# Infini-attention on one core: O formed with features on partitions

## The chip, the core and the metric

The kernel runs on one core of one Trainium2 chip. The core has a matrix engine (TensorE, PE in the profile; its weight loads are listed as PEld), three engines for elementwise work (VectorE or DVE, ScalarE or ACT, GpSimd or POOL), a sync engine (SP) that here issues nearly all transfers, and 16 DMA engines that carry them. The metric is device time in microseconds (us), lower is better. Three runs of the kernel before took 1043.05, 1041.55 and 1040.16 us, median 1041.55.

## The reference

Input `x` has 2048 tokens of 640 features. Two branches, A and B, each with weights of its own, apply the same memory-augmented attention to it, and a gate for each token mixes them. There are 32 heads of 20 features, and 4 segments of 512 tokens. Everything is float32.

```
q, k, v = x @ wq, x @ wk, x @ wv                # then cut into 32 heads and 4 segments
phi(t) = t + 1 if t > 0 else exp(t);  g = sigmoid(beta)          # one beta for each head
M = 0; z = 0
for each segment:
    p     = softmax(q k^T * 20**-0.5 + causal mask)
    a_dot = p v
    a_mem = (phi(q) M) / (phi(q) z + 1e-6)
    o     = g * a_mem + (1 - g) * a_dot
    M += phi(k)^T v;  z += sum of phi(k)
branch = o @ wo
gate = sigmoid(sum(x * gate_w));  out = gate * A + (1 - gate) * B
```

## The kernel before

The work is eight tiles: tile t is branch t % 2 of segment t // 2. A tile is cut into eight units of four heads, so 64 units in all, numbered 8t + u. TensorE's 128 rows are used as two halves of 64, each with a stream of its own; a product of 128 contracted rows is two records in the trace, one for each half. The 640 features are KT = 5 blocks of 128, the 512 tokens of a segment NB = 4 blocks of 128. Products that need more than the fast float format take three terms (high by high, high by low, low by high), so most operands are kept as a high and a low row.

The order of the work is set by a planner inside the program. It simulates the engines with a price for each instruction, and emits each engine's list in the order in which its own simulation comes to it. The table `RULES` gives for each unit the order of score and softmax pieces and how far they are spread. On the chip each engine works through its list in order, and waits by semaphores. Buffers are held in stores: eight banks of PSUM (128x512), `NBIG` = 27 rows of SBUF (128x512, called `row` in the trace), four quads each of q and k.

What a tile goes through, with the lines of the profile:

- Products of q, k, v and of the result (L643). q and k come out with features on partitions and go to DRAM (`qd`, `kd`, L625); from there SP loads them again by quads of four heads (`qst`, `kst`, L1032, 60 of 64 rows in each half). v goes to `vst[t % 2]`, tokens on partitions, 21 columns a head: 20 features and a one.
- Scores for the maxima (L1074), whose maxima VectorE takes (L1061). The maxima are turned (L1099), written into rows of `qst` (L1111), and the scores are formed once more, transposed (L1164), put through the exponential on ScalarE (L1156) and masked on GpSimd (L1157).
- PV (L1184): for each unit a bank with queries in the columns and, in four strips of 32 partitions, each head's 20 features and the row sum. The bank is copied to a row (L1209).
- `fin_unit`: four blocks, two halves, so eight transposes (L790) turn that row back to tokens on partitions; VectorE forms the weight gate x (1 - g) / row sum and multiplies (L1248 to L1250). For segments after the first GpSimd adds the memory's part (L1259).
- `mem_unit` (L752, from the third tile on): phi(q) x [M, z], for each of four token blocks and two groups of heads, with 128 tokens in the output's partitions and at most 84 columns per matmul. VectorE forms the weights, inverts them and multiplies into `Ot` (L766 to L769).
- `o_transpose`: for each of five blocks eight transposes (L790) turn O to features on partitions; it is split into high and low (L1277) for the product with wo.
- `back_unit` turns phi(k) (L790, L806), and `update_unit` adds phi(k)^T v to M and z (L830), held in `mbd`.

Where products are called for in a tile's stretch of the program is set by `window_jobs(t)`: first the rest of tile t's own products (`TAIL`), then the five O products of tile t - 1, then the first five of tile t + 1 (`HEAD`). Score, softmax, PV and transposing pieces are placed between them.

```
def window_jobs(t):
    got = [(t, kind, m) for kind, m in (TAIL if t else [("q", 1), ("k", 1), ("v", 0), ("q", 2), ("k", 2)] + TAIL[2:])]
    if t > 0:
        got += [(t - 1, "o", m) for m in range(KT)]
    if t < 7:
        got += [(t + 1, kind, m) for kind, m in HEAD]
    return got
```

Of the kernel before, what the change touches and what calls it, by code (L numbers as in the profile page):

```python
# [18 lines left out]
P = 128  # L19
# [15 lines left out]
OWN = [LO[m] if m == 0 else HI[m - 1] + 1 for m in range(KT)]  # L35

# [6 lines left out]
def tile_gated_mix_infini_attn(  # L43
# [47 lines left out]
        0: "TSTSTSTSTS 1.010 2.38 0.30 8",  # L91
        2: "TTSTSTSTSS 1.023 2.38 0.30 8",
        3: "TSTSTSTSTS 1.047 2.38 0.28 8",
        4: "TSTSTSTSTS 1.010 2.38 0.30 8",
        6: "TSSTTSSTTS 1.010 2.92 0.30 8",
        7: "TSTTSSTSTS 1.010 2.38 0.30 8",
        8: "TSTSTSTSTS 0.962 1.77 0.30 8",
        10: "TSTSTSTSTS 1.008 2.38 0.28 6",
        11: "TSTSTSTSTS 1.010 2.38 0.30 8",
        14: "TSTSTSTSTS 0.947 3.18 0.35 8",  # L100
        15: "TSTSTSTSTS 0.974 2.38 0.32 8",
        17: "TSSTTSSTTS 1.042 2.38 0.26 8",
        18: "TSTSTSTSTS 1.010 2.38 0.30 4",
        20: "TSTSTSTSTS 1.010 2.38 0.30 8",
        21: "SSTSTSTSTT 0.982 2.38 0.30 8",
        22: "TSTSTSTSTS 0.922 2.38 0.27 8",
        23: "TSTSTSTSTS 1.029 2.38 0.30 6",
        24: "TTSTSTSTSS 1.034 2.98 0.30 8",
        25: "TSTSTSTSTS 1.010 2.38 0.42 8",
        27: "SSTSTSTSTT 1.010 3.22 0.30 6",  # L110
        29: "TSTSTSTSTS 1.010 2.38 0.30 8",
        30: "SSSTSTSTTT 1.015 2.38 0.29 8",
        32: "TSTSTSTSTS 0.939 3.51 0.30 8",
        33: "TSTSTSTSTS 1.010 2.38 0.30 8",
        38: "TSTSTSTSTS 1.010 2.38 0.30 4",
        39: "TSTSTSTSTS 1.010 3.32 0.30 8",
        42: "STSTSTSTST 1.010 2.38 0.33 8",
        43: "TSTSTSTSTS 1.010 2.38 0.30 8",
        44: "TTSSTTSSTS 1.010 1.91 0.30 8",
        45: "TSTSTSTSTS 1.010 2.38 0.30 8",  # L120
        47: "TSTSTSTSTS 1.010 2.22 0.30 8",
        48: "TSTSTSTSTS 1.010 2.38 0.30 8",
        52: "TSTSTSTSTS 1.010 2.08 0.30 8",
        53: "SSTSTSTSTT 1.011 1.87 0.30 4",
        54: "TSTSTSTSTS 1.010 2.38 0.30 8",
        55: "TSTSTSTSTS 1.010 2.38 0.28 8",
        56: "TSTSTSTSTS 1.010 2.38 0.33 8",
        57: "TSTSTSTSTS 1.010 2.38 0.30 8",
        58: "TSTTSSTSTS 0.960 2.38 0.31 8",
        60: "TSTSTSTSTS 1.010 2.38 0.35 8",  # L130
        61: "TSTSTSTSTS 1.010 2.38 0.30 8",
        62: "TSTSTSTSTS 1.010 2.73 0.30 8",
        65: "TSTSTSTSTS 0.996 2.38 0.30 6",
    }
    rule = {}
    DONE = {"A": 0.14, "D": 0.11, "G": 0.1, "S": 0.0}
# [4 lines left out]
    def start_next(e):  # L141
# [7 lines left out]
        _, _, dur, emit, then = heapq.heappop(ready[e])  # L149
# [3 lines left out]
        def end():  # L153
            busy[e] = False
            load[e] -= dur
            if then:
                at(clk[0] + DONE[e], then)
            start_next(e)
# [10 lines left out]
    def put(e, dur, emit, then=None, prio=5):  # L169
        heapq.heappush(ready[e], (prio, next(seq), dur, emit, then))  # L170
        load[e] += dur
        start_next(e)
# [29 lines left out]
    lane = [0.0, 0.0]  # L202
    lane_ops = [deque(), deque()]
# [3 lines left out]
    def whole(dur, emit):  # L207
        now[0] = max(now[0], lane[0], lane[1]) + dur
        got = emit()
        lane[:] = [now[0], now[0]]  # L210
        advance(now[0])
        return got
# [4 lines left out]
    def op(half, dur, emit):  # L217
        now[0] = max(now[0], lane[half])
        advance(now[0])
        got = emit()  # L220
        lane[half] = now[0] + dur
# [44 lines left out]
    mbds = [[const.tile([P, HI[m] - LO[m] + 1, E1], F32, name=f"mbd{b}_{m}") for m in range(KT)] for b in range(2)]  # L266
# [1272 lines left out]
```

## Time and profile before

| | |
|---|---|
| median of three runs | 1041.55 us (1040.16 to 1043.05) |
| span of the profiled execution, the time that its page gives | 1041.1 us |
| granted TensorE clock | 1.000 |
| TensorE busy | 1031.4 us, 99% |
| VectorE, ScalarE, GpSimd busy | 759.5 (73%), 663.7 (64%), 583.9 (56%) us |
| share of TensorE in the chain that ended last | 94% |
| products L643 in that chain | 54% |
| PV L1184, L1164, L1074, transposes L790, updates L830, memory L752 in it | 14, 7, 7, 4, 3, 3% |
| moved by DMA, mean | 207.96 MB, 200 GB/s |

A busy share says how long an engine had something under way, not that it set the pace. Which engine did is read from the chain of waits: followed back from the last instruction, it names at each step what released it. A group of instructions is listed with its busy time, the mean length of one in ns, and the idle time of the engine ahead of it with what ended it. Since matmuls overlap, the length of one is more than its share of the time.

### The profile page before, as it was taken

To read this page: it belongs to the slowest core of one execution; us is meant where nothing else is said; L and a number is where in the kernel's file an instruction comes from. 1 tells how busy PE (TensorE), PEld (TensorE's weight loads), DVE (VectorE), ACT (ScalarE), POOL (GpSimd) and SP (SyncE) were. 2 spreads that over 40 slices of the span, in tenths; PEclk is the share of its full clock that TensorE was granted. 3 is DMA by queue.
4 is the path that set the end of the run, shared out by engine and by line. 5 is a ranking of instruction groups with operands and counts; after the bars stand their busy time and mean duration, and the time that the engine had idled before them with its cause. 6 is when DMAs were issued, how large, how long until landed. Compare 5 with 4: busy or idle time off the path is not lost.

```text
span 1041.1 us, 31911 instructions
## 1 busy us (share of the span) xinstructions
PE 1031.4 (99%) x11778; PEld 875.0 (84%) x11778; DVE 759.5 (73%) x2714; ACT 663.7 (64%) x1346; POOL 583.9 (56%) x1045
## 2 busy tenths in 40 slices
PE   9999999999999999999999999999999999999998
PEld 7887798888988889887898988988879888787876
DVE  4797877668776688776877768877578767788763
ACT  6376667667664576565857558666675756766581
POOL 4464646556364574556737467374764636655471
PEclk9999999999999999999999999999999999999999
DMA  8986687658574686655857477665685856857431
GB/s 270 309 277 166 204 244 221 189 176 258 150 229 130 199 267 181 223 160 160 271 154 227 129 215 251 200 212 155 203 250 156 256 157 195 265 159 225 127 118 52
DMA packets 110027, 207.96 MB, mean 200 GB/s; under 512 B 12464, under 2 KB 16560, under 8 KB 109872
## 3 DMA queue, kind: packets, MB, share of 16 engines
q1 hardware_dynamic: 109872, 205.93, 65.0%
q8 instruction: 93, 1.52, 0.6%
q14 instruction: 62, 0.51, 0.2%
HBM read 131.43 MB, written 73.40 MB: 197 GB/s over the span
## 4 chain that ended last, share of the span: by engine, by line
PE 94%; DMA 3%; ACT 1%; DVE 1%; SPq 0%; POOL 0%; issue 0%; ACTq 0%; DVEq 0%
PE bank L643 54%; PE bank L1184 14%; PE bank L1164 7%; PE bank L1074 7%; PE bank L790 4%; PE bank L830 3%; PE bank L752 3%; DMA kst<-kd 1%; DMA row<-in_xT_dram 1%; DMA wst<-in_a_wk_dram 1%; PE bank L691 1%; PE bank L1099 0%; DMA qd<-row 0%; PE bank L1003 0%; DVE row L988 0%
## 5 line engine op out<-in xcount | busy, mean ns | idle before, releaser
L1061 DVE CUSTOM_DVE_ANT_0 bank<-bank,tri 128x384 f32<-128x384 f32 (+3 forms) x1024 | 474.8, 518 | 163.3 <-PE bank L1074 137.6
L643 PE MATMUL bank<-row,wh 64*128 64x512 f32 x2308 | 518.4, 404 | 0.3
L1156 ACT ACTIVATE p<-bank 128x512 f32<-128x512 f32 x598 | 328.6, 599 | 143.2 <-PE bank L1164 104.9
L1157 POOL TENSOR_SCALAR_AFFINE_SELECT p<-p 128x256 f32<-128x256 f32 (+1 forms) x598 | 214.3, 367 | 264.2 <-ACT p L1156 251.6
L643 PEld LDWEIGHTS bank<-row,wh 64*128 64x128 f32 x2308 | 322.9, 185 | 14.6 <-issue 1.8
L643 PE MATMUL bank<-row,wl 64*128 64x512 f32 x1154 | 302.4, 400 | 0.0
L472 POOL TENSOR_TENSOR wl<-wst,wh 128x640 fp32r<-128x640 f32 x115 | 181.6, 1582 | 46.5 <-ACT wh L470 46.0
L643 PE MATMUL bank<-wvh,row 64*128 64x320 f32 x1280 | 192.7, 318 | 0.1
L643 PEld LDWEIGHTS bank<-row,wl 64*128 64x128 f32 x1154 | 173.6, 185 | 6.4 <-issue 1.4
L1074 PE MATMUL bank<-kst,qst 60*128 60x128 f32 (+3 forms) x1024 | 176.9, 320 | 2.0 <-DMA kst<-kd 1.3
L1164 PE MATMUL bank<-qst,kst 62*128 62x128 f32 (+3 forms) x1024 | 174.6, 318 | 0.0
L643 PEld LDWEIGHTS bank<-wvh,row 64*128 64x128 f32 x1280 | 153.4, 185 | 3.1 <-issue 1.6
L1184 PE MATMUL bank<-p,vst 128*32 128x512 f32 (+3 forms) x1948 | 145.3, 431 | 0.0
L1061 DVE DVE_READ_ACCUMULATOR2_ANT mx<- 128x1 f32 x1024 | 143.3, 140 | 0.0
L1164 PEld LDWEIGHTS bank<-qst,kst 62*128 62x128 f32 x1024 | 126.9, 186 | 8.8 <-issue 1.4
L1074 PEld LDWEIGHTS bank<-kst,qst 60*128 60x128 f32 x1024 | 125.3, 185 | 10.6 <-issue 3.0
L1184 PEld LDWEIGHTS bank<-p,vst 128*32 128x32 f32 x1948 | 58.3, 109 | 85.6 <-issue 63.6
L643 PE MATMUL bank<-wvl,row 64*128 64x320 f32 x640 | 107.9, 312 | 0.0
L470 ACT CAST wh<-wst 128x640 fp32r<-128x640 f32 x119 | 86.5, 736 | 19.0 <-PE bank L643 13.0
L1209 ACT COPY row<-bank 128x512 f32<-128x512 f32 x62 | 36.5, 588 | 79.0 <-PE bank L1184 74.4
L643 PEld LDWEIGHTS bank<-wvl,row 64*128 64x128 f32 x640 | 85.6, 185 | 0.4 <-issue 0.4
L790 PE MATMUL bank<-ident,row 64*128 64x64 f32 x752 | 75.4, 225 | 0.5 <-DVE mx L1061 0.2
(99 smaller groups left out, 1238.4 us busy)
## 6 DMA issues: line engine op xcount, KB each, us to landing
qd<-row SPq DMA_DIRECT2D x120, 256.0 KB
kd<-row SPq DMA_DIRECT2D x120, 256.0 KB
qst<-qd SPq DMA_DIRECT2D x128, 240.0 KB
kst<-kd SPq DMA_DIRECT2D x128, 240.0 KB
wst<-in_a_wq_dram SPq DMA_DIRECT2D x20, 320.0 KB
wst<-in_a_wk_dram SPq DMA_DIRECT2D x20, 320.0 KB
wst<-in_b_wq_dram SPq DMA_DIRECT2D x20, 320.0 KB
wst<-in_b_wk_dram SPq DMA_DIRECT2D x20, 320.0 KB
```

What stands on the lines that cost most here:

```text
L470: put("A", 0.66, lambda: nc.scalar.copy(wh, w3), lambda: put(lo_eng, lo_cost, lambda: lo.tensor_tensor(out=wl, in0=w3, in1=r32(wh), op=ALU ...
L472: lambda: lo.tensor_tensor(out=wl, in0=w3, in1=r32(wh), op=ALU.subtract), end, prio=3), prio=6)
L643: return nc.tensor.matmul(bank_of, lhsT=w[ROWS[half]], rhs=x_[ROWS[half]], start=start, stop=stop)
L752: return nc.tensor.matmul(pm[:, a - h0:c - h0, :].rearrange("p h e -> p (h e)"), lhsT=r32(pqTs[t, m][ROWS[half], P * n:P * (n + 1)]), rhs= ...
L790: return nc.tensor.transpose(px[:, n, r], block(n)[r], ident[r, r])
L1061: put("D", w / 960.0 + 0.112, lambda: nc.vector.tensor_tensor_reduce(out=sc[:, off:off + w], in0=sc[:, off:off + w], in1=tri[:, L - w:], s ...
L1074: lane_ops[half].append((w * 0.000458, lambda pair=pair, qb=qb, off=off, w=w, r=r, sc=sc: nc.tensor.matmul(sc[:, off:off + w], lhsT=q[r, p ...
L1156: put("A", 0.49, lambda: nc.scalar.activation(pt, sc, AF.Exp, scale=SCALE), lambda: (bank.give(sc), put("G", 0.05 + 0.16 * len(todo), lamb ...
L1157: "G", 0.05 + 0.16 * len(todo), lambda: nc.gpsimd.affine_select(out=blocks, in_=blocks, pattern=[[0, len(todo)], [1, P]], base=0, channel_ ...
L1164: lane_ops[half].append((w * 0.000458, lambda pair=pair, kb=kb, off=off, w=w, r=r, sc=sc: nc.tensor.matmul(sc[:, off:off + w], lhsT=k[r, p ...
L1184: nc.tensor.matmul(po[32 * j:32 * j + 32, P * kb:], lhsT=vst[t % 2][:, kb, h * E1:h * E1 + 32], rhs=pts[i, n, f][0][:, off:off + w], start ...
L1209: either(0.52, lambda: nc.scalar.copy(r32(oT), po), 0.63, lambda: nc.vector.tensor_copy(r32(oT), po), end, 2)
```

## The change

For tiles 0 to 6 nothing turns O back to tokens on partitions any more. The rows of PV leave with features on partitions and stay so:

- `rows_out`: a unit's PV row goes to DRAM (`od[t]`), and its four row sums into rows of an SBUF buffer `dens[t]` (32 heads x 512 tokens), both by DMA.
- `row_weights`: when all eight units of a tile are out, the tile's gates (`gd`, written to DRAM once a segment by `gate_rows`) are loaded into 32 partitions; VectorE multiplies row sums, gates and 1 - g, and inverts the 32x512 block.
- `mem_unit(t, g)` is turned round: M is the stationary operand and phi(q) with its 512 tokens the moving one, in six groups of 4 or 6 heads (`GROUPS`), so the output has up to 126 features on partitions. It is copied to a row and goes to DRAM (`md[t]`). `mem_weights` loads the z rows and gates into 32 partitions and inverts, as above.
- `scaled(t, k)`: for each of the five blocks of 128 features, the numerators come back from `od` or `md`, and the weights from the SBUF buffer, each head's row read 20 times; a block is cut where a head is cut, so up to three transfers for each. VectorE or GpSimd multiplies. Where memory is there, the two blocks are added. Two blocks of PV are in flight at a time, one of memory.
- `split_rows` makes the high and low rows for the product with wo.

Tile 7 keeps `fin_unit` and `o_transpose` for its PV part; its memory part comes by the new way. There is one v tile instead of two, and `job_v` waits for PV and updates of the tile before. `window_jobs` puts the five first products of tile t + 1 ahead of the O products of tile t - 1. `NBIG` goes from 27 to 42. The planner's prices and the table `RULES` are new, and with them the order of nearly all work.

```diff
     RULES = {
-        0: "TSTSTSTSTS 1.010 2.38 0.30 8",
+        0: "SSTSTSTSTT 0.985 2.38 0.33 6",
...
-    vst = [const.tile([P, NB, H * E1 + 12], F32, name=f"vst{i}") for i in range(2)]
+    vst = const.tile([P, NB, H * E1 + 12], F32, name="vst")
...
-    NBIG, NWST, NWH, SPARE = 27, 4, 4, 2
+    NBIG, NWST, NWH, SPARE = 42, 4, 4, 2
...
     def window_jobs(t):
...
+        ahead = [(t + 1, kind, m) for kind, m in HEAD] if t < 7 else []
+        n = 5
+        got += ahead[:n]
         if t > 0:
             got += [(t - 1, "o", m) for m in range(KT)]
-        if t < 7:
-            got += [(t + 1, kind, m) for kind, m in HEAD]
+        got += ahead[n:]
         return got
...
+    def gate_rows(s):
+        for b in range(2):
+            dma(0.5, lambda b=b: nc.sync.dma_start(
+                out=gd[b][s].rearrange("n p -> p n"), in_=gate[b][:, NB * s:NB * (s + 1)]),
...
-    def mem_unit(t, n, h):
+    def mem_unit(t, g):
...
+        def mm(half, m, a, c, start, stop):
             return nc.tensor.matmul(
...
+                b[(a - h0) * E1:(c - h0) * E1, :],
+                lhsT=mbd[m][ROWS[half], a - FROM[m]:c - FROM[m], :].rearrange("p h e -> p (h e)"),
+                rhs=r32(pqTs[t, m][ROWS[half], :]), start=start, stop=stop, skip_group_check=True,
             )
...
+                dma(0.75 * n / P, lambda: nc.sync.dma_start(
+                    out=md[t][h0:h1, :, :].rearrange("h e n -> (h e) n"), in_=r32(row[:n, :])), sent, prio=-1)
...
+    def mem_weights(t, den, gat):
...
+            nc.vector.tensor_scalar(g, g, gmp[b][:, 0:1], None, op0=ALU.mult)
+            nc.vector.scalar_tensor_tensor(out=d, in0=d, scalar=1e-6, in1=g, op0=ALU.add, op1=ALU.mult)
+            nc.vector.reciprocal(d, d)
...
     def job_v(t, half):
-        yield from hold_on(lambda: t < 2 or oTs_begun[t - 2] == 8 and all((t - 2, m) in upd_done for m in range(KT)), "v")
+        ms = range(KT) if half else range(3)
+        yield from hold_on(lambda: t < 1 or oTs_begun[t - 1] >= 4 + 4 * half and (
+            t > 6 or all((t - 1, m) in upd_done for m in ms)), "v")
...
+    def rows_out(i, oT):
...
+            dma(0.25, lambda: nc.sync.dma_start(out=dens[t][4 * u:4 * u + 4, :], in_=rows[:, DH, :]), both, prio=-1)
+            dma(0.75, lambda: nc.sync.dma_start(
+                out=od[t][4 * u:4 * u + 4, :, :].rearrange("h e n -> (h e) n"), in_=r32(oT)), both, prio=-1)
...
+    def row_weights(t, gat):
...
+                nc.vector.scalar_tensor_tensor(out=den, in0=den, scalar=gdp[b][:, 0:1], in1=gat_, op0=ALU.mult, op1=ALU.mult)
+                nc.vector.reciprocal(den, den)
...
+    def scaled(t, k, num, wb, kind="o", more=None):
...
+            anyof(1 if kind == "o" else 4, ready_, D=(0.65, lambda: nc.vector.tensor_tensor(out=num, in0=num, in1=wb, op=ALU.mult)),
+                  G=(1.255, lambda: nc.gpsimd.tensor_tensor(out=num, in0=num, in1=wb, op=ALU.mult)))
...
+                hs = slice(h, h + n // DH)
+                ways = ((num, src_n[hs, :DH, :]), (wb, src_w[hs, None, :].to_broadcast([n // DH, DH, L])))
+            for dst, src in ways:
+                dma(0.75 * n / P, lambda dst=dst[p0:p0 + n, :], src=src: nc.sync.dma_start(out=dst, in_=src), all_, prio=-1)
```

Two places of the engines' lists show what moves. The first is TensorE's list in the middle of tile 2's memory product, between its v products; in a row stand the line, the operation, the output, its operands and the output's shape. Before, it reads:

```order
L752 MATMUL bank_118<-mbd_3_73,row_5247_4796 128x84
L752 MATMUL bank_122<-mbd_4_74,row_5653_5165 128x84
L752 MATMUL bank_118<-mbd_4_74,row_5653_5165 128x84
L752 MATMUL bank_121<-mbd_2_72,row_4625_4184 128x21
L752 MATMUL bank_120<-mbd_3_73,row_5247_4796 128x84
L752 MATMUL bank_121<-mbd_3_73,row_5247_4796 128x84
L752 MATMUL bank_120<-mbd_4_74,row_5653_5165 128x84
L752 MATMUL bank_121<-mbd_4_74,row_5653_5165 128x84
L643 MATMUL bank_124<-wvh,row_3652_3355 128x320
L790 MATMUL bank_119<-ident,row_5538_5042 128x64 x2
```

And after the change, where the same product has line 802 and the projections line 708:

```order
L802 MATMUL bank_147<-row_5465_4588,mbd_3_73 126x512
L802 MATMUL bank_142<-row_5769_4832,mbd_4_74 84x512
L708 MATMUL bank_146<-wvh,row_2803_2451 128x320
L708 MATMUL bank_140<-wvh,row_2803_2451 128x320
L708 MATMUL bank_146<-wvh,row_2826_2467 128x320
L708 MATMUL bank_140<-wvh,row_2826_2467 128x320
L708 MATMUL bank_146<-wvh,row_2878_2501 128x320
L708 MATMUL bank_140<-wvh,row_2878_2501 128x320
L802 MATMUL bank_142<-row_5769_4832,mbd_4_74 84x512
L802 MATMUL bank_147<-row_5465_4588,mbd_3_73 126x512
L708 MATMUL bank_146<-wvh,row_2917_2527 128x320
L802 MATMUL bank_147<-row_5769_4832,mbd_4_74 126x512
```

Many short matmuls into banks with tokens on partitions have become a few with 512 columns, into banks with features on partitions, and the v products stand between them.

The second place is SP's list, behind the last PV row of tile 6, where the row buffers, the writes of q and k (`kd`, `qd`) and the quads for the last units are issued. Before:

```order
L625 DMA kd_112<-row_17310_15701 128x512 x2
L625 DMA kd_112<-row_17311_15702 128x512
L625 DMA qd_104<-row_17317_15706 128x512 x2
L625 DMA qd_104<-row_17318_15707 128x512
L1111 DMA qst_82<-mr_148 2x8x128 x2
L478 DMA wst_126<-in_a_wo_dram 128x640
L1032 DMA qst_80<-qd_104 60x2x512 x2
L1032 DMA kst_84<-kd_112 60x2x512 x2
```

After the change, from the load of the gate row (`gd`) and the first two blocks of tile 6 on (`od_125` holds its PV rows, `row_16905_13286` its weights):

```order
L1373 DMA row_19186_14962<-gd_3_135 32x512
L542 DMA wst_151<-in_a_wo_dram 128x640
L1417 DMA row_19291_15043<-od_125 120x1x512
L1417 DMA row_19292_15044<-row_16905_13286 120x1x512
L1417 DMA row_19291_15043<-od_125 8x512
L1417 DMA row_19292_15044<-row_16905_13286 8x1x512
L1417 DMA row_19299_15046<-od_125 12x512
L1417 DMA row_19300_15047<-row_16905_13286 12x1x512
L1417 DMA row_19299_15046<-od_125 100x1x512
L1417 DMA row_19300_15047<-row_16905_13286 100x1x512
L1417 DMA row_19299_15046<-od_125 16x512
L1417 DMA row_19300_15047<-row_16905_13286 16x1x512
```

The transfers of a block's numerators and of its weights are new in SP's list, four or six for a block, and stand in the queue among the writes and the quads.

More of the change, by code (lines that the diff above doesn't have):

```diff
@@ L575, in later @@
         late.sort(key=lambda x: x[:2])
-    Ot = {}
-    O_store = Store([sb.tile([P, NB, D], F32, tag=f"O{i}", name=f"O{i}", bufs=1) for i in range(2)])
+    O7 = []
     OTs = {}
@@ new lines, in done, with want_mem_weights @@
+        def done():
+            for m in range(KT):
+                if g in READERS[m]:
+                    pq_left[t, m] -= 1
+                    if not pq_left[t, m]:
+                        big.give(pqTs.pop((t, m)))
+            big.want((F32,), got, prio=2)
+        return split_unit(*ops, done)
+    mem_out = set()
+    def want_mem_weights(t):
+        if t > 1 and t in rows_there and all((t, g) in mem_out for g in range(len(GROUPS))):
+            mem_ready.add(t)
+            mem_rows()
@@ L786, in turn @@
+    wmem = {}
     def turn(px, block):
```

564 lines of the change are left out of this document (340 added, 224 removed).

## The prediction

> **What bounds the kernel now.** I read the page from the top, then the chain of waits, the groups kept apart by shape, stretches of the timeline, and the DMA views.
>
> ```profile
> span 1041.1 us, 31911 instructions
> PE 1031.4 (99%) x11778; PEld 875.0 (84%) x11778; DVE 759.5 (73%) x2714; ACT 663.7 (64%) x1346; POOL 583.9 (56%) x1045
> DMA  8986687658574686655857477665685856857431
> PE 94%; DMA 3%; ACT 1%; DVE 1%; SPq 0%; POOL 0%; issue 0%; ACTq 0%; DVEq 0%
> ```
>
> TensorE is busy in 99% of the span and is 94% of the chain that ended last; no other engine is above 73%. So work taken off TensorE's list should shorten the kernel nearly one for one, as long as what replaces it arrives in time. Only the last two slices (31 and less in the DMA line, about 50 us) have the DMA engines quiet. The span, 1041.1 us, lies 0.45 us below the median of the three runs (1041.55); I count from the span and let the difference go, since I call anything within 0.3% (3.1 us) no change.
>
> The array works as two halves of 64 rows, each with its own stream. A group's mean is the length of one instruction, not its share of the clock, so the pace has to come from stretches where one kind follows itself:
>
> ```profile
> 739.05 0.40 PE L790 MATMUL bank<-ident,row 64*128 64x64 f32 x4
> 405.82 1.61 PE L752 MATMUL bank<-mbd,row 64*128 64x84 f32 x25
> 830.26 1.62 PE L752 MATMUL bank<-mbd,row 64*128 64x84 f32 x20
> 100.21 1.21 PE L830 MATMUL bank<-vst,row 64*128 64x147 f32 x16
> 729.49 1.33 PE L830 MATMUL bank<-vst,row 64*128 64x147 f32 x16
> 821.51 2.36 PE bank L1184 x32
> ```
> ```profile
> L790 PE MATMUL bank<-ident,row 64*128 64x64 f32 x752 | 75.4, 225 | 0.5 <-DVE mx L1061 0.2
> L790 PE MATMUL bank<-ident,O 64*128 64x64 f32 x320 | 35.8, 225 | 0.1
> L752 PE MATMUL bank<-mbd,row 64*128 64x84 f32 x432 | 45.0, 276 | 0.1
> L752 PE MATMUL bank<-mbd,row 64*128 64x63 f32 x48 | 8.4, 259 | 0.0
> L752 PE MATMUL bank<-mbd,row 64*128 64x21 f32 x48 | 8.3, 249 | 0.0
> L830 PE MATMUL bank<-vst,row 64*128 64x147 f32 x384 | 51.9, 292 | 0.0
> ```
> ```profile
> 0.00:1041.10 1041.10, 107.69 (x1072) 91.89 (x1072) 1.00 0.66 200
> ```
>
> The first fence is the timeline (start, length, instructions merged) with one line of the chain; the second the groups; the third is L790 alone over the whole span.
>
> **TensorE, removed: transposes.** Counted in the two instruction lists, 1072 of 64x64 become 344: 728 fewer, 364 in each half. Four in one half take 0.40 us and the last lasts 0.225, so (0.40 - 0.225)/3 = 0.058 us each at full pace; the union of all 1072 is 107.69 us, 0.100 each, which counts waits and the ends too. 364 x 0.058 = 21.1 and 364 x 0.100 = 36.4. I take 0.075, nearer the pace: **-27.3 us**.
>
> **TensorE, removed and added: the memory product.** The old form is 264 matmuls, two records each (432 + 48 + 48 = 528). Both halves together go at (1.61 - 0.276)/24 = 0.056 to (1.62 - 0.276)/19 = 0.071 us a record: 29.4 to 37.4 us in all. I take 0.060, **-31.7 us**. The new form is 84 matmuls, 42 in each half, with 512 moving columns and up to 126 stationary ones. No row shows it. The nearest by tile is the update (L830): sixteen records in both halves are eight in a row, (1.21 - 0.292)/7 = 0.131 to (1.33 - 0.292)/7 = 0.148 us for 147 columns, 0.89 to 1.01 ns a column; two records of 512 are 0.91 to 1.03 us, and 42 of them 38.3 to 43.4. The nearest by length is PV: its 1280 columns, two records each and four side by side, take 2.36 us with the start, 0.92 ns a column at most and about 0.8 without the ends: 34 us. I take **+38**: the streams are as long as PV's, in the tile of the update. The product itself gets no cheaper; fewer instructions are eaten up by four times the columns.
>
> Together -27.3 - 31.7 + 38 = **-21.0 us** (bounds -36.4 - 37.4 + 34 = -39.8, and -21.1 - 29.4 + 43.4 = -7.1). Products (L643), scores (L1074, L1164), PV (L1184) and updates (L830) keep their counts and shapes.
>
> **The other engines.** Removed from VectorE are 56 rounds of fin_unit's three instructions and 48 of the memory's; added are 85 multiplies, adds and subtractions of whole rows, 17 copies, and 13 gate calculations on 32x512.
>
> ```profile
> L494 DVE TENSOR_TENSOR row<-row,row 128x512 fp32r<-128x512 f32 x5 | 3.3, 691 | 1.3 <-ACT row L490 1.3
> L1250 DVE TENSOR_TENSOR ft<-bank,fw 128x320 f32<-128x320 f32 x48 | 23.6, 492 | 4.6
> L768 DVE RECIPROCAL mw<-mw 128x19 f32<-128x19 f32 x24 | 6.6, 276 | 0.8
> L768 DVE RECIPROCAL mw<-mw 128x13 f32<-128x13 f32 x24 | 5.8, 240 | 1.0 <-DVE mw L766 0.2
> L494 POOL TENSOR_TENSOR row<-row,row 128x512 fp32r<-128x512 f32 x15 | 19.3, 1288 | 1.2 <-ACT row L490 0.9
> L1259 POOL TENSOR_TENSOR O<-O,ft 128x320 f32<-128x320 f32 x48 | 42.0, 876 | 43.2 <-DVE ft L1250 32.9 <-DVE mw L766 3.9 <-DMA kst<-kd 2.4
> DVE bank L1061 <- PE bank L1074: 137.6, 135, 4.4
> ```
>
> 85 x 0.691 = 59 us comes against some 95 us that go; with the copies and the gate work VectorE's sum hardly moves. POOL loses 42 and gains 45 x 1.288 = 58. ACT gains 27 evacuations of about 0.6. All stay below 80% of the span, so the sums cost nothing; what can cost is one long instruction. From 13 to 19 elements a reciprocal grows by 36 ns, 6 ns an element, so 512 need about 0.16 + 3.07 = 3.2 us, against 0.7 if it ran like a plain row. VectorE's list is in order: behind it stand the maxima of L1061, which free the score banks. VectorE waits 137.6 us for scores now, which is the cover. Without cover 13 x (3.2 - 0.7) = 33 us would pass to TensorE; with it nothing. I take 2 us, since the banks are eight.
>
> [...]
>
> **The way of O.** For tiles 0 to 6 the quotient now leaves by DMA, comes back in blocks, and only then is divided, added and split. TensorE waits for it at the O product of that tile. Adding up TensorE's list at these prices, the first O product stands about 60 us behind the last PV of its tile for tiles 0 to 5, since five products of the next tile were put ahead of it, and about 38 us for tile 6, which has none. In that time lie the last rows out, the gate row, VectorE's 3.9 us, five blocks of two transfers, two blocks in flight, then about 3 us of multiply, add and split. If a block's transfers take 4 us, five are 20 and the whole chain some 35 to 45 with the transfers between: covered for tiles 0 to 5, up to 10 us late for tile 6. I take 2. The single v tile adds a wait of job_v for the other stream's PV and updates; in TensorE's list these stand ahead of it in any case, so it costs nothing unless an update is late, when the 17.6 us of v products behind it shift as a whole.
>
> Sum: 1041.1 - 21.0 + 2 + 2 = **1024 us**. Own range 1008 to 1037.
>
> **The transfers.** Their load is the main threat.
>
> ```profile
> DMA packets 110027, 207.96 MB, mean 200 GB/s; under 512 B 12464, under 2 KB 16560, under 8 KB 109872
> q1 hardware_dynamic: 109872, 205.93, 65.0%
> qst<-mr SPq DMA_DIRECT2D x128, 8.0 KB
> qst<-qd SPq DMA_DIRECT2D x128, 240.0 KB
> 487.00:489.00 2.00, 2.00 (x32) 0.78 (x24) 1.36 (x8) 0.00 (x0) 0.61 (x1) 1.00 1.02 232
> 496.00:498.00 2.00, 2.00 (x24) 1.86 (x22) 1.82 (x8) 1.52 (x3) 2.00 (x4) 1.00 1.02 380
> 485.31 0.87 SPq L1032 DMA_DIRECT2D kst<-kd  x2
> 495.10 1.40 SPq L625 DMA_DIRECT2D qd<-row  x3
> ```
>
> The small packets tell on how many of the 16 engines a transfer runs. Two loads of beta make 256; the other 12,208 are exactly 507 x 16 + 256 x 15 + 128 x 2, one for each engine of each transfer, if the 256 loads of 60 rows use 15 engines and the 128 of mr (16 rows to 2) use two. By the same pattern the new blocks of 120 = 6 x 20 rows use six engines and those of 100 = 5 x 20 use five. Now each engine is busy 65.0% of 1041 = 677 us. At full rate a 2 KB packet takes 16 x 2048/(380/1.02) = 88 ns; over the whole run 677 x 16 us/100,550 = 108 ns. An engine that takes part in all the new transfers gets 448 packets of PV rows, 288 of memory rows, 13 x 200 = 2600 of blocks and weights, and some 300 of rests: about 3,640, or 320 to 393 us. If all are at the same five engines these carry 997 to 1070 us; evenly spread, the added 59 MB bring every engine to about 840 us.
>
> [...]
>
> **Rivals.**
> A, the TensorE sum holds and the transfers stay hidden: 1024 us, chance 0.50. For it: the chain has 3% DMA now, quads are loaded as soon as their buffers come free, and part of the 677 us is waiting, since quad loads go at 232 GB/s where writes go at 380.
> B, the new order also removes present waits of TensorE (the pieces of the chain are cut at hundreds of places): at the transposes' upper price, 36.4 instead of 27.3, and with 7 us of waits gone, 1008 us. Chance 0.08. Against it: nothing in the trace says that a new order has fewer waits.
> C, the engines that carry the blocks become the bound, from the point where they need more than the 1020 us less the quiet 50 to 60: 997 + 60 = about **1,060 us**, slower. Chance 0.24. For it: the exact count above; against it: the wait would need the same engines each time, and the loads stand a unit ahead.
> D, O comes late at every tile and VectorE's 3.2 us go uncovered: 10 + half of 33 us eat the gain: about 1,041 us, no change. Chance 0.09.
> E, the weights are read from one partition per head, 20 times each, and these reads throttle each other. Quad loads and writes show such a loss: 16 x 2048/(232/1.02) = 144 ns a packet against 88. [...] Chance 0.09; no row shows such reads.
>
> [...]
>
> **How the numbers follow.** Faster by more than 3.1 us: A and B, 0.58. Within: D, 0.09. Slower: C and E, 0.33. The time is A's, 1024 us. The range goes from 1006, just under B, to 1085, which takes in D and nearly all of C and leaves out E; about 0.18 lie outside.
>
> **What would show it.** Right: TensorE near 99% of a span of 1010 to 1035 us, L802 with 168 records at about 0.4 us each, 344 transposes, and no wait of TensorE above 3 us at L708 for a row that L1425 to L1427 wrote. C: idle time of TensorE behind qst, kst or O rows, and a DMA share with the mean well below 1 in stretches where transfers are late. E: the row<-row transfers far longer than the row<-od ones. D: RECIPROCAL on 32x512 of 3 us with score banks waiting behind it. I am wrong on the size if the 512-column product costs more than 43 us or the transposes gave less than 21.

## The result: slower by 42%

The changed kernel takes 1481.63 us (four runs, 1474.7 to 1484.75) against 1042.3 us before: a ratio of 1.4204, 95% interval 1.4161 to 1.4247. The forecast was 1024 us, with a range up to 1085. The page of the changed kernel, from the lines that answer to those shown of before:

```profile
span 1477.5 us, 30281 instructions
PE 1164.0 (79%) x10690; PEld 932.9 (63%) x10690; DVE 787.4 (53%) x2509; ACT 672.9 (46%) x1359; POOL 601.2 (41%) x1040
PEclk9899977999698898788987998869989698896978
...
PE 13%; DMA 9%; SPq 9%; DVE 3%; issue 2%; ACT 1%; POOL 0%; POOLq 0%; DVEq 0%; ACTq 0%
PE bank L708 7%; DMA row<-row 6%; SPq L1417 6%; PE bank L1286 2%; PE bank L1261 1%; PE bank L1171 1%; DMA row<-gd 1%; DVE bank L1158 1%; DMA qst<-qd 1%; SPq L1208 1%; SPq L814 0%; SPq L1129 0%; DMA kst<-kd 0%; PE bank L802 0%; SPq L690 0%
```

TensorE was 94% of the chain before. Now the chain can be followed back only to 923 us, so its shares add up to 37%; of these TensorE has 13, and the weights' transfers (`row<-row`) with SP's issuing of blocks (L1417) have 12. TensorE stands still for 313.5 us (1477.5 - 1164.0; before 9.7). It is also busy for 132.6 us more than before (1164.0 - 1031.4) although it has fewer instructions. The line of the clock shows why: it was full speed throughout and is now below nine tenths in about half of the slices (mean 0.870). The trace's clock record holds 56 stretches at half speed, 3.4 to 17 us long, 382 us together; 268 us of them fall on busy time, so 134 us are lost. Idle and clock add up to the whole difference: 1041.1 + (313.5 - 9.7) + 134 = 1479. That leaves no room for the 21.0 us that TensorE was to save; the last part comes back to it.

What TensorE waits for is read in two steps, from the view of waits:

```profile
DVE row L1388 <- DMA row<-row: 228.5, 35, 15.2
DVE bank L1158 <- PE bank L1171: 194.7, 145, 12.5
...
POOL row L1389 <- DMA row<-row: 121.0, 17, 14.3
...
PE bank L1261 <- DVE mx L1158: 75.1, 19, 12.5
...
PE bank L1171 <- DVE mx L1158: 56.3, 16, 10.7
...
PE bank L1286 <- DVE mx L1158: 14.1, 4, 8.3
...
PE bank L708 <- DVE mx L1158: 13.0, 3, 5.5
```

Columns are the sum in us, the times, the longest. The four rows in which TensorE waits for maxima (`mx`) add up to 158.5 us, half of its idle time; the other half is spread over some thirty rows, none above 15 us. VectorE's multiply (L1388) and GpSimd's (L1389) wait for `row<-row`, the transfers that spread the weights. The maxima (L1158) stand behind these multiplies in VectorE's list. The longest case, in the timelines of VectorE, TensorE and SP (start, length; in brackets the idle time before and what ended it), and in two stretches (the stretch and its length, the busy us of PE, PEld, DVE, ACT and POOL with their instructions, the clock, the DMA share, GB/s):

```profile
1343.61 0.14 DVE L1158 DVE_READ_ACCUMULATOR2_ANT mx<- 128x1 f32 x1
1356.61 0.69 DVE L1388 TENSOR_TENSOR row<-row,row 128x512 f32<-128x512 f32 x1 [12.86 <-DMA kst<-kd]
1357.22 0.29 DVE L1158 CUSTOM_DVE_ANT_0 bank<-bank,tri 128x128 f32<-128x128 f32 x1
```
```profile
1357.62 0.79 PE L1261 MATMUL bank<-qst,kst 62*128 62x512 f32 x2 [12.48 <-DVE mx L1158]
```
```profile
1347.40 0.79 SPq L1417 DMA_DIRECT2D row<-row  x1
1348.23 0.49 SPq L1417 DMA_DIRECT2D row<-od  x1
1348.77 2.45 SPq L1417 DMA_DIRECT2D row<-row  x1
1351.32 3.64 SPq L814 DMA_DIRECT2D md<-row  x1
```
```profile
1344.00:1357.00 13.00, 1.14 (x16) 0.87 (x12) 0.39 (x1) 0.62 (x1) 4.47 (x5) 0.71 0.38 88
1357.00:1365.00 8.00, 7.38 (x58) 4.14 (x59) 3.57 (x10) 3.15 (x7) 1.31 (x4) 0.62 0.88 260
```

VectorE sits 12.86 us at one multiply (L1388 reads blocks alone, so the `kst<-kd` in brackets is only the transfer that landed at that time). TensorE stops for 12.48 us, and in the 8 us after it the clock is 0.62. Meanwhile the DMA engines are at 0.38 and 88 GB/s. So they are not short of capacity as a whole; the next runs ask what is slow. SP too is held: an issue that takes 0.4 us elsewhere takes 2.5 and 3.6.

### The profile page after: what moved, and what is told of

It is laid out like the page before. It is cut to its first block, busy times and chain, and to the rows that moved or that the text cites. A ratio compares the mean times of both kernels' runs of the same rounds, so it can differ in the third digit from the quotient of the medians.

```text
span 1477.5 us, 30281 instructions
## 1 busy us (share of the span) xinstructions
PE 1164.0 (79%) x10690; PEld 932.9 (63%) x10690; DVE 787.4 (53%) x2509; ACT 672.9 (46%) x1359; POOL 601.2 (41%) x1040
## 2 busy tenths in 40 slices
DMA packets 147608, 266.61 MB, mean 180 GB/s; under 512 B 21376, under 2 KB 25472, under 8 KB 147456
## 5 line engine op out<-in xcount | busy, mean ns | idle before, releaser
L1158 DVE CUSTOM_DVE_ANT_0 bank<-bank,tri 128x256 f32<-128x256 f32 (+3 forms) x1024 | 475.3, 517 | 249.4 <-PE bank L1171 194.7
L708 PE MATMUL bank<-row,wh 64*128 64x512 f32 x2308 | 574.5, 428 | 18.2 <-ACT row L822 5.9
L1253 ACT ACTIVATE p<-bank 128x512 f32<-128x512 f32 x538 | 297.1, 600 | 187.8 <-PE bank L1261 164.5
L708 PEld LDWEIGHTS bank<-row,wh 64*128 64x128 f32 x2308 | 354.3, 199 | 44.0 <-issue 6.7
L708 PE MATMUL bank<-row,wl 64*128 64x512 f32 x1154 | 333.8, 423 | 0.0
L1261 PE MATMUL bank<-qst,kst 62*128 62x384 f32 (+3 forms) x1024 | 200.1, 354 | 127.6 <-DVE mx L1158 75.1
L1171 PE MATMUL bank<-kst,qst 60*128 60x384 f32 (+3 forms) x1024 | 200.5, 348 | 82.9 <-DVE mx L1158 56.3
L708 PE MATMUL bank<-wvh,row 64*128 64x320 f32 x1280 | 225.1, 348 | 23.9 <-ACT row L822 8.9
L708 PEld LDWEIGHTS bank<-wvh,row 64*128 64x128 f32 x1280 | 183.9, 212 | 31.2 <-ACT row L822 9.1
L708 PEld LDWEIGHTS bank<-row,wl 64*128 64x128 f32 x1154 | 192.0, 199 | 8.0 <-issue 1.4
L1388 DVE TENSOR_TENSOR row<-row,row 128x512 f32<-128x512 f32 x45 | 32.3, 718 | 285.7 <-DMA row<-row 228.5
L1286 PE MATMUL bank<-p,vst 128*32 128x384 f32 (+3 forms) x1812 | 166.9, 480 | 13.1 <-POOL p L1254 6.6
L1158 DVE DVE_READ_ACCUMULATOR2_ANT mx<- 128x1 f32 x1024 | 142.7, 139 | 0.0
L708 PE MATMUL bank<-wvl,row 64*128 64x320 f32 x640 | 131.3, 348 | 0.0
L708 PEld LDWEIGHTS bank<-wvl,row 64*128 64x128 f32 x640 | 103.9, 218 | 1.0 <-issue 0.4
```

The lines of the kernel that those rows point to most:

```text
L708: return nc.tensor.matmul(bank_of, lhsT=w[ROWS[half]], rhs=x_[ROWS[half]], start=start, stop=stop)
L1158: put("D", w / 960.0 + 0.112, lambda: nc.vector.tensor_tensor_reduce(out=sc[:, off:off + w], in0=sc[:, off:off + w], in1=tri[:, L - w:], s ...
L1171: lane_ops[half].append((cost_r(w), lambda pair=pair, qb=qb, off=off, w=w, r=r, sc=sc: nc.tensor.matmul(sc[:, off:off + w], lhsT=q[r, pair ...
L1253: put("A", 0.493, lambda: nc.scalar.activation(pt, sc, AF.Exp, scale=SCALE), lambda: (bank.give(sc), put("G", 0.137 + 0.118 * len(todo), l ...
L1261: lane_ops[half].append((cost_r(w), lambda pair=pair, kb=kb, off=off, w=w, r=r, sc=sc: nc.tensor.matmul(sc[:, off:off + w], lhsT=k[r, pair ...
L1286: nc.tensor.matmul(po[32 * j:32 * j + 32, P * kb:], lhsT=vst[:, kb, h * E1:h * E1 + 32], rhs=pts[i, n, f][0][:, off:off + w], start=(kb == ...
```

## The experiments

**Paces and packets by themselves.** One kernel carried out only the shapes in question.

> No attention in this one: it only carries out transfers and matmuls of the shapes in question, each kind several times in a row, and its output is not the reference's. Transfers wait for the one before. If reading one partition many times is what is slow, a 2 KB packet of the broadcast from 6 neighbouring partitions takes about 0.29 us as in the changed kernel where only it was under way, and 0.084 us from DRAM with the same six engines. If it is the neighbourhood of the partitions, the same broadcast from partitions 20 apart is near 0.09. If it is only the crowding of six engines in the full kernel, all are near 0.084 here. TensorE: 30 matmuls of 512 columns by 126 in each half at 0.91 to 1.03 us a pair by my estimate from the update, 0.8 to 0.92 by PV; 60 of 84 columns in each half at 0.11 to 0.14 us a pair. VectorE: reciprocal of 32x512 at 3.3 us.

Its SP timeline, four transfers of a kind in a row, each after the one before it has landed; then TensorE's:

```profile
32.40 25.86 SPq L83 DMA_DIRECT2D to<-w  x4
...
138.23 10.99 SPq L91 DMA_DIRECT2D to<-w  x4
151.89 10.87 SPq L93 DMA_DIRECT2D to<-w  x4
...
182.62 12.79 SPq L97 DMA_DIRECT2D to<-wd  x4
```
```profile
19.43 25.91 PE L111 MATMUL bank<-r,r 64*126 64x512 f32 x120
45.18 13.52 PE L114 MATMUL bank<-r,r 64*128 64x84 f32 x240
```

L83 is the changed kernel's broadcast, six neighbouring partitions to 120 rows: 8.4 us from one to the next ((25.86 - 0.7)/3). From partitions 20 apart (L91) it is 3.4, four apart (L93) 3.4, from DRAM (L97) 4.0. The packet records say the same: a median of 0.295, 0.084, 0.084 and 0.084 us, so from six neighbours a packet takes 3.5 times as long. With 16 neighbouring partitions on all 16 engines it was 0.296. So it is neither SBUF as such nor six engines, but reading neighbours over and over. In the changed kernel 2,408 packets of 2 KB lie between 0.27 and 0.32 us, against 170 before; with the weights spaced, in a run below, they are 371. Broadcast packets number 13 x 5 x 128 = 8,320, so not all of them are that slow: with six neighbours alone, half of the packets took 0.295 us or more and a quarter 0.16 or less.

On TensorE the 60 new matmuls take 25.91 us, 0.432 each, so 84 are 36.3 us. The 120 old ones take 13.52 us, 0.056 a record, so 528 records are 29.7. The reciprocal of 32x512 took 3.33 us.

**How much hangs on the weights' transfers.** Three kernels with the changed kernel as the base: no weights loaded; weights read from DRAM; weights spread on the way to DRAM.

```diff
# e1
-            for dst, src in ways:
+            for dst, src in ways[:1]:
# e2
+            dma(0.25, lambda: nc.sync.dma_start(out=wd["o", t], in_=den), gone, prio=-1)
# e3
+            dma(3.75, lambda: nc.sync.dma_start(out=wd["o", t], in_=den[:, None, :].to_broadcast([H, DH, L])), gone, prio=-1)
...
+        dma(0.75, lambda: nc.sync.dma_start(out=wb, in_=src_w[P * k:P * (k + 1), :]), all_, prio=-1)
```

> The weights are inverted but not loaded into blocks; each block is multiplied by itself, so the output is not the reference's. All else, the numerators' 169 transfers on five and six engines too, stays. If the broadcast reads are the cause (theory 1): 1,030 to 1,070 us. If it is the crowd of transfers on few engines and in SP's queue whatever their source (theory 2): half of the transfers are left and so is about half of the loss, 1,200 to 1,300 us.

> The inverted weights are written to DRAM once (32 rows) and the same 169 broadcast transfers, cut in the same places and on the same five and six engines, read them there. Theory 1 (reading a few SBUF partitions over and over): the packets go at 0.084 to 0.09 us, 1,030 to 1,090 us. Theory 2 (few engines, SP's queue): nothing changes but one more transfer, 1,400 us or more.

> The weights are written to DRAM 20 times over in one transfer of 640 rows, and each block loads 128 rows of them in one piece. So the broadcast is on all 16 engines, 13 transfers a tile become 6, and no weight transfer is on few engines. Theory 1: as e2, 1,030 to 1,080 us, if the writes (reading 32 partitions, two for each engine) are not slow in turn. Theory 2: far below e2, 1,100 to 1,200, with the numerators' part left.

Measured: 1160.3 us (one run), 1278.9 (ratio 1.2277, 1.2223 to 1.2331) and 1242.9 (1.1931, 1.1897 to 1.1966). The first two lie between the two theories, the third above the ranges of both. The source of the reads is worth about 200 us; 237 us above the kernel before stay with quick packets, and 118 with no weights loaded at all. Neither theory is whole.

**Three single edits and two together.** The planner told the true price; the weights four partitions apart; the gate rows turned on TensorE; the last two at once.

```diff
# e6
+                late_ = 1.1 + (min(n, DH) * 0.293 if dst is wb else min(n, DH) * 0.084)
+                dma(0.75 * n / P, lambda dst=dst[p0:p0 + n, :], src=src: nc.sync.dma_start(out=dst, in_=src), all_, prio=-1, lat=late_)
# e7
-            dma(0.25, lambda: nc.sync.dma_start(out=dens[t][4 * u:4 * u + 4, :], in_=rows[:, DH, :]), both, prio=-1)
+            dma(0.25, lambda: nc.sync.dma_start(out=dens[t][16 * u:16 * u + 16, :], in_=rows[:, DH, None, :].to_broadcast([4, 4, L])), both, prio=-1)
# e8
-                out=gd[b][s].rearrange("n p -> p n"), in_=gate[b][:, NB * s:NB * (s + 1)]),
+        ops = [[((0.02, 0.056, 0.056), lambda a, z, r=r: nc.tensor.transpose(bk[:NB, r], g[r], ident[r, r]))] for r in ROWS]
```

> Only the planner's price of the block transfers changes: a broadcast's packets are told to take 0.293 us each and land that much later, so VectorE's and GpSimd's multiplies stand later in their lists. If the loss is the wrong place of the multiplies in the lists (work behind them waits in order): 1,150 us or less. If the transfers themselves are too slow, TensorE waits at the products with O instead, and SP's queue is as full: 1,300 us or more.

> The weights lie four partitions apart (head h on partition 4h, the three between hold copies), with the same transfers, engines and byte counts. By the micro run the packets go at 0.084 in place of 0.295 us. If the neighbourhood of the partitions is what costs: as with the weights in DRAM, 1,240 to 1,290 us. If it was reading SBUF at all: no change, 1,450 or more.

> Only the gate rows change: TensorE turns a segment's gates (4 columns) into 4 rows, which go out in packets of 512 B, in place of eight transfers of 512 single numbers each. If each of these transfers holds up the others for some 5 to 10 us, as the long packets behind them suggest: 40 to 80 us less, 1,400 to 1,440 us. If they are harmless: 1,475 to 1,485 us.

> Spaced weights and turned gate rows together. If the two causes add up: 1,180 to 1,230 us; what is left above 1,024 us is then the block transfers on five and six engines and SP's longer list. If the gates matter only while the weights are slow: as e7, 1,240 to 1,290.

Measured: 1404.9 (one run), 1288.0 (1.2372, 1.2336 to 1.2408), 1458.2 (one run) and 1270.9 (1.2207, 1.2168 to 1.2246). Spacing takes off 194 us, the neighbourhood's own price. The true price, and with it a later place of the multiplies in the lists, takes off 77 by itself. The gate rows take off 23 alone (one run) and 17 beside the spacing, less than the 40 to 80 expected; together (1270.9) they miss the 1,180 to 1,230 us expected if the causes add up. What their transfers do is seen near the start of the changed kernel (SP, ScalarE, TensorE):

```profile
53.09 0.43 SPq L613 DMA_DIRECT2D gd<-gate  x1
53.57 1.50 SPq L518 DMA_DIRECT2D wst<-in_a_wv_dram  x3
```
```profile
65.83 0.72 ACT L508 CAST wvh<-wst 128x640 fp32r<-128x640 f32 x1 [10.57 <-DMA wst<-in_a_wv_dram]
```
```profile
68.37 0.36 PE L886 MATMUL bank<-ident,row 64*128 64x64 f32 x1 [10.15 <-ACT p L1253]
```

Behind the 512 single numbers of one gate row, loads of 2.5 KB packets take up to 6.8 us a packet; the v weights issued at 53.57 reach ScalarE at 65.83, and TensorE stops for 10 us. Packets of 2 to 8 KB that took over 1.5 us number 136 in the changed kernel, 6 with the gate rows turned on TensorE and 1 in the kernel before.

**What is left with quick packets.** From the last kernel on: more margin in the planner; whole blocks (weights spread to DRAM, numerators packed there by one transfer a tile, each block two transfers of 128 rows); both; and, to see the floor, no blocks at all (there the weights need no spacing).

```diff
# e10
+                dma(0.75 * n / P, lambda dst=dst[p0:p0 + n, :], src=src: nc.sync.dma_start(out=dst, in_=src), all_, prio=-1, lat=6.1)
# e11
+        dma(3.75, lambda: nc.sync.dma_start(out=nd["o", t], in_=od[t][:, :DH, :]), both_, prio=-1)
...
+        for dst, src in ((num, src_n), (wb, src_w)):
+            dma(0.75, lambda dst=dst, src=src: nc.sync.dma_start(out=dst, in_=src[P * k:P * (k + 1), :]), all_, prio=-1)
# e13
-        all_ = then_all(2 * len(pieces), there)
+        there()
```

> As the run with spaced weights and turned gate rows, but the planner is told that each block transfer lands 5 us later, so the multiplies stand later in VectorE's and GpSimd's lists. If what is left is VectorE waiting at the head of its list for blocks that come later than the planner believes: 1,271 falls to 1,080 to 1,150 us. If it is SP's queue and the few engines: 1,230 or more.

> Spaced weights and turned gate rows; the weights go to DRAM 20 times over, the numerators are packed in DRAM by one transfer a tile, and each block is two transfers of 128 rows on all 16 engines in place of four or six on a few. If few engines and the number of transfers are what is left: 1,080 to 1,150 us. If it is the planner's belief about the landing: 1,230 or more.

> The last two together: whole blocks, and a planner that is told 5 us more. If both the few engines and the place in the lists matter: 1,030 to 1,080 us. If it comes out as one of them alone, that one was the cause.

> All block transfers are left out: nothing is loaded, the multiplies work on a constant, so the output is not the reference's. Rows of PV and memory still go out, weights are still formed and inverted, TensorE's list is complete, and the gate rows are turned by TensorE. If the sum for TensorE is right (20.7 us less by the paces of the micro run) and the block transfers are the whole rest of the loss: 1,018 to 1,035 us. If the new order, the single v tile or the long reciprocals cost by themselves: 1,060 or more.

Measured: 1204.4 (one run), 1155.8 (1.1097, 1.1035 to 1.1158), 1163.0 (1.1166, 1.1101 to 1.1231), and 1123.5 (one run). VectorE's multiply with the idle time ahead of it, in the groups: the changed kernel, spaced weights, with margin, and whole blocks.

```profile
L1388 DVE TENSOR_TENSOR row<-row,row 128x512 f32<-128x512 f32 x45 | 32.3, 718 | 285.7 <-DMA row<-row 228.5 <-DMA qd<-row 15.3 <-DMA row<-od 13.1
```
```profile
L1388 DVE TENSOR_TENSOR row<-row,row 128x512 f32<-128x512 f32 x45 | 36.6, 812 | 130.7 <-DMA row<-row 63.5 <-DMA kst<-kd 17.1 <-DMA wst<-in_a_wk_dram 8.8
```
```profile
L1406 DVE TENSOR_TENSOR row<-row,row 128x512 f32<-128x512 f32 x55 | 42.9, 780 | 50.1 <-DMA row<-row 39.5 <-DMA wst<-in_b_wq_dram 5.2 <-DMA kst<-kd 4.3
```
```profile
L1414 DVE TENSOR_TENSOR row<-row,row 128x512 f32<-128x512 f32 x41 | 39.9, 974 | 14.9 <-DMA row<-wdm 7.9 <-DMA row<-wdo 3.5 <-issue 2.5
```

The idle time falls from 285.7 to 14.9 us, and the time with it. Blocks of four to six pieces on few engines cost 115 us in the planner's order (1270.9 to 1155.8), of which margin alone wins 66 (one run); with whole blocks margin wins nothing. The pieces, the engines and SP's list (1405 transfers, then 1223) change together here and are not told apart. The floor came as a surprise: 1123.5 without any block is 100 us above the sum for TensorE. In that kernel TensorE stops at twelve of the 13 reciprocals for 1.3 to 8.2 us, and at the other for 0.7. One of them, in the timelines of VectorE and TensorE and the stretches around it:

```profile
448.05 1.83 DVE L1374 SCALAR_TENSOR_TENSOR row<-row,gdp,row 32x512 f32<-32x512 f32 x1
449.91 3.34 DVE L1375 RECIPROCAL row<-row 32x512 f32<-32x512 f32 x1
453.18 0.66 DVE L1176 CUSTOM_DVE_ANT_0 bank<-bank,tri 128x512 f32<-128x512 f32 x1
```
```profile
455.17 0.80 PE L1189 MATMUL bank<-kst,qst 60*128 60x512 f32 x2 [2.83 <-DVE mx L1176]
```
```profile
440.00:448.00 8.00, 7.91 (x79) 6.96 (x78) 7.08 (x23) 5.73 (x12) 5.43 (x8) 1.00 0.71 257
448.00:452.00 4.00, 4.00 (x55) 2.38 (x51) 3.97 (x3) 1.01 (x2) 3.02 (x3) 1.00 0.71 192
452.00:460.00 8.00, 3.18 (x19) 2.29 (x17) 6.67 (x12) 1.74 (x4) 4.58 (x3) 0.64 0.34 95
```

5.2 us of weights go ahead of the maxima; TensorE stops for 2.83 us, and its clock is 0.64 in the next stretch. The planner had priced multiply and reciprocal at 1.25.

**The reciprocals.** Left out of the kernel without blocks, and made short in the full one, by laying a tile's row sums out as 128x128.

```diff
# e15
-                nc.vector.reciprocal(den, den)
# e14
-        den, gat_ = dens[t], gat
+        den, gat_ = dens[t][:, :P], gat[:, :P]
```

> As the run without block transfers (1,123.5 us), and without the 13 reciprocals of 32x512 (the weights stay uninverted; the output is not the reference's). In that run TensorE stands still for 1.3 to 8.2 us at each of the 13 and its clock is halved for a while behind it. If the uncovered reciprocals are the rest of the loss: 1,035 to 1,060 us and a clock of 0.99 or more. If it is the new order or the single v tile: 1,100 or more.

> As the run with whole blocks (1,156 us), but the row sums of a tile lie as 128x128 (head h's tokens in four partitions) in place of 32x512 with copies, so multiply and reciprocal take about 1.2 us in place of 4.2 to 4.9. The weights go out in four transfers of packets of 512 B. If the long reciprocal holds up the maxima: 70 us less, 1,080 to 1,100 us. If it is only in the way where something else is late: 1,140 or more.

Measured: 1086.6 (one run, against 1123.5) and 1120.6 (1.0744, 1.0688 to 1.08, against 1155.8). They cost 37 and 35 us, not the 70 expected; in the full kernel the weights also go out in four transfers instead of one. A reciprocal of 128x128 takes 0.953 us.

**VectorE and GpSimd, and the order of O.** On the version with short reciprocals: all work on blocks on GpSimd, or O ahead of the next tile's products as before the change. Then the floor once more with GpSimd alone, and a little margin for the best version.

```diff
# e16, e19
-            anyof(1 if kind == "o" else 4, ready_, D=(0.65, lambda: nc.vector.tensor_tensor(out=num, in0=num, in1=wb, op=ALU.mult)),
-                  G=(1.255, lambda: nc.gpsimd.tensor_tensor(out=num, in0=num, in1=wb, op=ALU.mult)))
+            anyof(1 if kind == "o" else 4, ready_, G=(1.255, lambda: nc.gpsimd.tensor_tensor(out=num, in0=num, in1=wb, op=ALU.mult)))
# e17
+        n = 0
# e18
+            dma(0.75, lambda dst=dst, src=src: nc.sync.dma_start(out=dst, in_=src[P * k:P * (k + 1), :]), all_, prio=-1, lat=3.6)
```

> As the run with short reciprocals (1,121 us), but all multiplies, adds and subtractions of the blocks are on GpSimd, none on VectorE. In that run VectorE's 87 of them take 0.84 to 1.02 us on average and up to 2.05, against 0.69 alone, and stand ahead of the maxima while they wait for blocks. If VectorE's list is what is left: 1,060 to 1,085 us. If GpSimd (1.27 us each, ahead of the masks) becomes what PV waits for: 1,130 or more.

> As the run with short reciprocals (1,121 us), but the O products of a tile stand ahead of the next tile's first products again, as before the change. By my count of TensorE's list the slack of the O chain falls from some 60 to some 40 us for tiles 0 to 5. If the chain now fits in 40 us: within 1,110 to 1,130 us, and the new order of the jobs is worth nothing. If it needs the 60: 1,150 or more.

> The best full version so far (1,109 us: whole blocks, short reciprocals, blocks on GpSimd), with a planner that is told each block lands 2.5 us later. If GpSimd still waits for blocks ahead of masks: 1,085 to 1,100 us. If the late landing no longer matters: within 1,100 to 1,120.

> As the run without block transfers and reciprocals (1,086.6 us), and with the blocks' multiplies, adds and subtractions on GpSimd alone; the output is not the reference's. If VectorE's waiting for GpSimd (1.1 us in place of 0.69 for 81 operations) is what is left above TensorE's sum of 1,020: 1,035 to 1,055 us. If it is the order itself: 1,075 or more.

Measured: 1108.7 (1.0637, 1.0555 to 1.0719), 1164.4 (1.1171, 1.1079 to 1.1263), 1119.2 (1.0738, 1.0643 to 1.0833) and 1056.5 (one run). Handing the blocks to GpSimd takes off 12 us in the full version (runs of 1105 and 1112 against 1119 and 1122) and 30 in the floor (1086.6 to 1056.5); the margin on top of it takes nothing off. The order with O first costs 44 us, and there TensorE waits for O itself, in the kernel's waits:

```profile
PE bank L729 <- ACT row L1447: 26.4, 16, 5.6
```

Why VectorE gains from handing the blocks over is seen in the kernel without blocks, line by line (count, then least, median and longest in ns): L1406 and L1435 read two operands from SBUF, L695 one from PSUM.

```profile
L1406 DVE TENSOR_TENSOR row<-gw x38: 616/675/1792, 186.1 to 1083.9; 128x512 f32<-128x512 f32 x38
```
```profile
L1435 DVE TENSOR_TENSOR row<-row,row x27: 668/774/2049, 187.8 to 1108.8; 128x512 fp32r<-128x512 f32 x27
```
```profile
L695 DVE TENSOR_TENSOR row<-bank,row x80: 667/692/693, 16.1 to 1027.6; 128x512 fp32r<-128x512 f32 x80
```

The ones with two operands in SBUF take up to 2.0 us, 1.3 more than alone, which is about the length of one GpSimd multiply (1.29 us in the kernel before); the others never take more than 0.693. The changed way of O gives VectorE 81 operations with two operands in SBUF in this kernel, and all 30 of them that took over 0.8 us overlap a GpSimd instruction that reads SBUF.

No version beats the kernel before; the best full one, 1108.7 us, is still 6% slower.

## Why the prediction was wrong, by its own steps

**The step that failed is the term of 2 us for the way of O.** It put a block's transfers at 4 us and took them as hidden behind some 60 us of TensorE's work. The weights of a block of 120 rows alone take 8.4 us as the kernel reads them, and 4.0 from DRAM. The wait did not come at the O products either, where it was looked for: VectorE's multiplies waited for the weights (228.5 us) ahead of the maxima, and TensorE for the maxima. The cause was on the list as rival E, reads from one partition per head. In the micro run a packet of such a read took 0.295 us at the median and 0.16 or less in a quarter of the cases; the prediction had worked out 0.144 for a quad load, and from partitions four apart it is 0.084. E got a chance of 0.09 because no row showed such reads, although the quad loads showed a loss (232 GB/s against 380 for the writes). E names the reads alone; the multiplies' place in VectorE's list and the half speed of TensorE behind its stops (134 us) are not in it.

**"The transfers stay hidden" (rival A)** failed without E too. With quick packets and turned gate rows the kernel takes 1271 us, and whole blocks give 115 back. Rival C came near it with blocks on few engines (the changed kernel's 21,376 packets under 512 B add up with six engines for a transfer of 120 rows and five for one of 100; which engines these are no run shows), but priced them by their load; with margin alone winning 66 of the 115, how late a block lands against the place of its multiply counts for more than half. The DMA share was 0.38 in the longest stop.

**TensorE's sum** held in the two terms that were measured by themselves: new product +36.3 for +38, old one -29.7 for -31.7. The transposes were not; at the price taken for them the sum is -27.3 - 29.7 + 36.3 = -20.7 for -21.0. No whole kernel shows it. The pages of the floor (1056.5 us) and of the best full version (1108.7) have TensorE busy for 98% of the span again:

```profile
PE 1037.5 (98%) x10706; PEld 859.2 (81%) x10706; DVE 679.0 (64%) x2404; ACT 670.7 (64%) x1374; POOL 704.3 (67%) x1125
```
```profile
PE 1078.7 (98%) x10706; PEld 874.8 (79%) x10706; DVE 685.2 (62%) x2417; ACT 677.6 (61%) x1374; POOL 699.7 (63%) x1125
```

Of these 6.8 and 32.8 us are at half speed, so at full speed they are 1034.1 and 1062.3 us, and 1030.0 in the changed kernel, against 1031.4 before. Busy time counts while either half has something under way, so a half that waits alone hides in it. That the saving was lost in such waits is a reading; no run shows it.

**VectorE's long reciprocal** was sized right, 3.34 us for 3.2, and wrongly covered: I took 2 us, and it costs 35 to 37. The bound without cover, 33, was near it. The 137.6 us in which VectorE waits for scores did not serve as cover; that TensorE needs each maximum soon after its score is my reading, and no run tries it.

**The slack of the O chain**: with O first, the slack that I counted as some 40 us was not enough even with quick whole blocks. In the changed kernel's own order the view of waits lists no wait at L708 for a row of O above 3 us, as I asked for; but that sign was too narrow, since the loss sat with the scores.

**Not in the sum at all**: the clock, the gate rows (17 to 23 us), what blocks on VectorE cost beside GpSimd (12 us in the full version, 30 in the floor).

What stays open is the 36 us between the floor and the sum (1056.5 against 1020.4). About 11 of them are idle time (17.2 for 9.7 us) and clock (3.4); the rest lies inside TensorE's busy time, and no run tells the new list, the single v tile, GpSimd's longer list or the transposes' price apart. The 52 us between the best version and the floor are block transfers and short reciprocals together, not told apart either; with them the DMA engines are busy for 84.9% of the span, against 65.0% before the change, which no run tests.

## What to carry to other kernels

Where an engine's list is in order, a new instruction that waits for a transfer holds all that is queued behind it (12.86 us in the longest case here): ask what stands behind it, and price the transfer at its landing, not at its bytes. Here the source of a broadcast wanted its rows apart: neighbouring partitions read many times cost 3.5 times as much a packet (0.295 us against 0.084). In this kernel, which kept TensorE busy without a gap, the stops were paid for again in the clock (134 us beside 304 of idle time), so a long instruction on another engine is hidden only if what it delays has slack of its own. And a TensorE that is 98% busy need not be as quick as before: compare its busy time, not its share.

## What the runs showed of the hardware that was not expected

- In the kernel without blocks the clock was halved in eleven stretches, 68 us in all. Nine of them, of 3.4 to 10.2 us, came within 5 us of the start of a stop of TensorE of 2.2 to 3.3 us, and one of 13.7 us in a stop of 8.2; ahead of the last, of 6.8 us, there was none above 0.3. Four stops of 1.3 to 2.1 us were not followed by one.
- A transfer that spreads a single partition to 20 rows took 0.476 us a packet (median), more than six neighbours together to 120 rows (0.295).
- One transfer of 512 single numbers to DRAM slowed other packets to 1.5 to 6.8 us for some 10 us; with the gate rows turned on TensorE such packets all but vanished (6 for 136).
- SP's issue of a transfer, 0.4 us at the median before and after the change, took up to 2.1 us before and up to 4.6 after; over the run SP spent 999 us issuing 1405 transfers, 757 us for as many with the weights spaced, and 408 us for 891 before.
